# Merged loads, a rebalanced first batch and keep-warm matmuls in a spectral-mixing and MLP kernel on one core

## The chip, the cores and the metric

The kernel runs on one core of a Trainium2 chip. The metric is device time in microseconds (us) for one execution, taken as the median of several executions. A ratio is always the mean time of one kernel's runs over the mean of the other kernel's runs of the same rounds. It is therefore not quite the ratio of the medians that are quoted beside it. Intervals are 95%.

Engine names in the profile: PE is the tensor engine (matmul), PEld its weight loads, DVE the vector engine, ACT the scalar engine, POOL the GpSimd engine, SP the sync engine that issues stores.

## The reference

There are eight sequences of 3008 tokens with 256 channels. Each is filtered in the frequency domain along the tokens, and an MLP with a leaky ReLU of slope 0.01 follows. Inputs and output are float32; the kernel works in float16 with float32 sums.

```python
def _attn_ref(x, filt_r, filt_i):            # x: 8 x 3008 x 256
    X = np.fft.rfft(x, axis=1)
    F = (filt_r + 1j * filt_i)[None, :, :]   # 1505 x 256
    y = np.fft.irfft(X * F, n=x.shape[1], axis=1)
    return y.astype(np.float32)

def _moe_ref(x, w_in, w_out):                # x: 24064 x 256, w_in: 256 x 2048
    h = x @ w_in
    g = np.maximum(0.01 * h, h)
    return (g @ w_out).astype(np.float32)
```

## The kernel before

The transform of 3008 points is split as 94 x 32 (`N1` x `N2`). For each batch there is a first DFT over `n1` (matmuls with `f1_sb`), a transpose on DVE (`t1_part`), a second DFT over `n2` with the product by the filter, an inverse over `n2`, another DVE transpose (`t2_part`), and the last inverse DFT (`sb_group`) into `yts`. The MLP then runs in chunks of 512 tokens: `moe1_group` makes `h` on PE and its gate on ACT, and `moe2_slice` makes the output. Batches 1 to 7 are transformed beside the MLP of the batch ahead. Batch 0 has nothing to run beside, so it has its own path, in two halves of 128 channels each, and that path is what the change is about. Here are its loads, its steps and its order.

```python
def x_load(b, n0=0, nn=N2, d0=0, dn=D):
    src = x[b].rearrange("(n1 n2) d -> n1 n2 d", n2=N2)
    for lo, cnt in ((0, 64), (64, N1 - 64)):              # two transfers: 64 and 30 rows
        nc.gpsimd.dma_start(x_sb[lo : lo + cnt, ds(n0, nn), ds(d0, dn)],
                            src[lo : lo + cnt, ds(n0, nn), ds(d0, dn)])

def filt_load(dst, src, d0, dn):
    h = N2 // 2
    for s in range(2):                                    # four transfers of 16 rows
        q = s * Q
        nc.gpsimd.dma_start(
            dst[q : q + h, :, ds(d0, dn)], rows(src, NC * s, N1, 1, h, NC, d0, dn))
        nc.gpsimd.dma_start(
            dst[q + h : q + Q, :, ds(d0, dn)], rows(src, N1 - NC * s, N1, -1, h, NC, d0, dn))
# ... [cut] ...
def first_s2(hf, g, on_pool):                             # second DFT and products, 8 k1 columns
    ps = php.tile([P, W, DH], FP32, tag="ph", name=f"f2_h{hf}_g{g}")   # php: two PSUM slots
    # ... [two matmuls into ps] ...
    if on_pool:
        # ... [xs, y allocated] ...
        for j in range(2):
            nc.scalar.copy(xs[j][:], ps[:, ts(j, 4), :])  # ACT copies, POOL multiplies
        for i in range(2):
            for j in range(2):
                nc.gpsimd.tensor_tensor(y[i][:, ts(j, 4), :], xs[j][:], fs[i][:, ts(j, 4), :], AL.mult)
    else:
        # ... [y allocated] ...
        for i in range(2):
            nc.vector.tensor_tensor(y[i][:], ps[:], fs[i], AL.mult)    # DVE reads PSUM

def upper(hf):                                            # filter to the upper partitions
    for t, cp in ((fa_sb, nc.scalar.copy), (fb_sb, nc.vector.tensor_copy)):
        cp(t[64:P, :, ts(hf, DH)], t[0:64, :, ts(hf, DH)])

ac = (nc.scalar.copy, nc.scalar.copy)
first_front(0, copies)                                    # first DFT of a half, then t1
upper(0)
first_s2(0, 0, False), first_s2(0, 1, True)
first_s2(0, 2, False)
first_sa(0, 0, ac)                                        # inverse over n2
first_front(1, ac)
x_load(1)
first_sa(0, 2, ac), first_sa(0, 1, ac)
upper(1)
first_s2(1, 0, False), first_s2(1, 1, True)
# ... [w_out load] ...
first_s2(1, 2, False)
first_sa(1, 0, ac)
for i in range(2):
    t2_part(0, i)()
first_sa(1, 2, ac), first_sa(1, 1, ac)
for i in range(2, 4):
    t2_part(0, i)()
for g in range(16):                                       # last inverse DFT
    sb_group(0, g, copies[g % 2 if g >= 8 else 0], two[(g // 2) % 2])()
```

## Time and profile before

| | before |
|---|---|
| median of the first job's runs | 794.77 us (794.16 to 795.11, 4 runs) |
| profiled span | 793.3 us |
| first moe matmul / first gate activation | 45.70 / 47.60 us |
| transposes of batch 1 start | 61.09 us |
| last output copy starts | 789.04 us |

PE is busy for 96% of the span, and by the prediction's reading everything that can move lies ahead of about 68 us. The prediction, two sections on, shows the busy shares, the windows and the chain of work. These are the waits in the stretch from 26 to 36 us before the change: the engine and line that waited, what released it, then the total in us, the number of waits and the longest.

```profile
POOL fy_h_g L267 <- ACT fx_h_g L264: 4.1, 1, 4.1
DVE big L189 <- ACT big L177: 3.9, 1, 3.9
...
PE f_h_g L257 <- ACT fx_h_g L264: 1.6, 1, 1.6
DVE fy_h_g L271 <- ACT fa_sb L290: 1.4, 1, 1.4
```

DVE waits twice in this stretch, once for ACT's casts (3.9 us) and once for ACT's copy of the filter (1.4 us).

### The profile page before, as it was taken

How to read it: one execution, taken by the hardware profiler on the slowest of the kernel's cores; microseconds unless marked ns; L12 is line 12 of the kernel's file. 1: busy time of each engine (PE TensorE's matmuls, PEld its weight loads, DVE VectorE, ACT ScalarE, POOL GpSimd, SP SyncE). 2: the span in 40 equal slices, each digit the busy share in tenths (PEclk: the TensorE clock that was granted, in tenths of full speed). 3: DMA queues.
4: the chain of work that ended last, by engine and by line, in shares of the span. 5: the costliest groups of instructions: out<-in, count | busy, mean ns of one | idle time of the engine just before them, and what ended most of it. 6: DMA issues, size and time to landing. Idle time of an engine off the chain costs nothing.

```text
span 793.3 us, 13469 instructions
## 1 busy us (share of the span) xinstructions
PE 762.5 (96%) x5740; PEld 526.6 (66%) x5740; DVE 361.3 (46%) x448; ACT 561.2 (71%) x804; POOL 158.3 (20%) x138
## 2 busy tenths in 40 slices
PE   3688999999999999999999999999999999999997
PEld 2255677666776667866778667776677666676665
DVE  4728751675407743376414763077431765200000
ACT  3786768777596766877677776877769676666663
POOL 8763500141002500033000420024000340000000
PEclk9889999999999999999999999999999999999999
DMA  9934100501114010410105010151100101101111
GB/s 174 206 46 91 37 32 27 119 29 38 42 40 99 33 40 28 89 57 28 40 28 118 27 41 34 34 108 38 41 27 28 40 27 41 40 28 40 40 40 54
DMA packets 42300, 43.16 MB, mean 54 GB/s; under 512 B 14574, under 2 KB 40814, under 8 KB 41582
## 3 DMA queue, kind: packets, MB, share of 16 engines
q0 software_dynamic: 16048, 16.76, 13.0%
q1 hardware_dynamic: 26192, 25.53, 9.2%
q8 instruction: 45, 0.74, 0.4%
q14 instruction: 15, 0.12, 0.1%
HBM read 33.64 MB, written 24.64 MB: 73 GB/s over the span
## 4 chain that ended last, share of the span: by engine, by line
PE 91%; ACT 4%; DVE 3%; DMA 1%; issue 0%; POOL 0%; ACTq 0%; DVEq 0%; POOLq 0%
PE po_ps L348 40%; PE h_c_g L334 40%; PE sb_b_g L233 3%; PE s_b_g L166 3%; PE s_b_g L206 2%; PE sa_b_g L221 2%; ACT big L177 2%; DVE big L189 1%; DVE big L197 1%; PE o_c_t L348 1%; DMA x_sb<-in_x_dram 1%; ACT gt_c L339 1%; DVE fy_h_g L271 1%; PE f_h_g L257 0%; ACT fa_sb L290 0%
## 5 line engine op out<-in xcount | busy, mean ns | idle before, releaser
L339 ACT ACTIVATE gt_c<-h_c_g 128x1024 f16<-128x1024 f32 x376 | 385.6, 1026 | 196.7 <-PE h_c_g L334 195.7
L334 PE MATMUL h_c_g<-yt,w_in_sb 128*128 128x512 f16 (+7 forms) x1728 | 387.6, 352 | 1.3 <-ACT gt_c L339 1.0
L348 PE MATMUL po_ps<-w_out_sb,gt_c 128*128 128x256 f16 x2944 | 381.4, 272 | 0.6 <-ACT ost_c_t L355 0.6
L348 PEld LDWEIGHTS <-gt_c 128*128 128x128 f16 x3008 | 290.6, 98 | 88.7 <-issue 3.8
L334 PEld LDWEIGHTS <-w_in_sb 128*128 128x128 f16 x1728 | 163.3, 98 | 96.7 <-issue 2.8
L214 POOL TENSOR_TENSOR y_b_g<-p_b_g,p_b_g 128x512 f16<-128x512 f32 x84 | 106.9, 1273 | 222.3 <-DVE p_b_g L212 222.3
L189 DVE STREAM_TRANSPOSE big<-big 128x1024 f32<-128x1024 f32 x32 | 55.7, 1844 | 145.8 <-ACT big L177 145.7
L236 DVE CAST yt<-sb_b_g 128x376 f16<-128x376 f32 x116 | 58.5, 545 | 90.4 <-PE sb_b_g L233 90.2
L210 DVE TENSOR_TENSOR p_b_g<-s_b_g,fa_sb 128x512 f32<-128x512 f32 x84 | 58.1, 692 | 37.3 <-PE s_b_g L206 33.0
L355 ACT COPY ost_c_t<-po_ps 128x256 f32<-128x256 f32 x184 | 69.4, 377 | 7.4 <-PE po_ps L348 6.3
L197 DVE STREAM_TRANSPOSE big<-big 128x1024 f32<-128x1024 f32 x32 | 58.4, 1937 | 34.2 <-ACT big L177 34.2
L122 POOL DMA_DIRECT2D x_sb<-in_x_dram x22 | 13.9, 637 | 263.2 <-PE s_b_g L166 262.3
L177 ACT CAST big<-s_b_g 128x512 f16<-128x512 f32 x112 | 61.5, 621 | 0.0
L211 DVE TENSOR_TENSOR p_b_g<-s_b_g,fb_sb 64x512 f32<-64x512 f32 x84 | 58.2, 693 | 1.1
L212 DVE TENSOR_TENSOR p_b_g<-s_b_g,fb_sb 64x512 f32<-64x512 f32 x84 | 57.4, 684 | 1.1
L177 ACT CAST big<-sa_b_g 128x512 f16<-128x512 f32 x84 | 50.6, 602 | 0.0
L233 PEld LDWEIGHTS <-big 128*128 128x128 f16 x512 | 29.7, 101 | 17.7 <-DVE big L197 3.8
L233 PE MATMUL sb_b_g<-i_sb,big 128*128 128x94 f16 x512 | 33.3, 210 | 3.6 <-DVE big L197 3.2
L166 PE MATMUL s_b_g<-x_sb,f_sb 94*128 94x256 f16 x224 | 35.0, 276 | 1.3 <-ACT big L177 0.5
L206 PE MATMUL s_b_g<-big,small_sb 128*128 128x512 f16 x84 | 31.8, 379 | 1.8 <-DVE big L189 1.8
L221 PE MATMUL sa_b_g<-y_b_g,small_sb 128*128 128x512 f16 x84 | 31.8, 379 | 0.0
L166 PEld LDWEIGHTS <-f_sb 94*128 94x128 f16 x224 | 21.3, 99 | 11.9 <-issue 4.0
(37 smaller groups left out, 135.3 us busy)
## 6 DMA issues: line engine op xcount, KB each, us to landing
out_dram<-ost_c_t SPq DMA_DIRECT2D x92, 256.0 KB, 2.1
x_sb<-in_x_dram POOLq DMA_DIRECT2D x7, 1024.0 KB, 8.0
x_sb<-in_x_dram POOLq DMA_DIRECT2D x7, 480.0 KB, 10.2
x_sb<-in_x_dram POOLq DMA_DIRECT2D x4, 256.0 KB, 6.2
w_in_sb<-in_moe_w_in_dram POOLq DMA_DIRECT2D x1, 1024.0 KB, 9.6
w_out_sb<-in_moe_w_out_dram POOLq DMA_DIRECT2D x1, 1024.0 KB, 9.7
f_sb<-fwd_const SPq DMA_DIRECT2D x4, 192.0 KB, 3.4
fa_sb<-in_filt_r_dram POOLq DMA_DIRECT2D x8, 96.0 KB, 6.2
```

The lines of the kernel that those rows point to most:

```text
L166: nc.tensor.matmul(ps[:, j, :], f1_sb[:N1, n2, :], x_sb[:N1, n2, :], start=True, stop=True)
L177: copy(paired(dst)[:, ds(n0, nn), ds(e0, de)], ps[:].rearrange("p n (e t) -> p n e t", t=2))
L189: nc.vector.transpose(o, a)
L197: nc.vector.transpose(o[:, i // 2, ts(i % 2, E4), :], a)
L211: nc.vector.tensor_tensor(p2[0:64], ps[64:P], fb[64:P], AL.mult)
L214: nc.gpsimd.tensor_tensor(y1[:], p1[:], p2[:], AL.add)
L233: nc.tensor.matmul(ps[:, j, :], src[:, dt, n2, :], i1_sb[:, n2, :], start=True, stop=True)
L236: copy(yv[:, :, ds(4 * h, 4)], ps[:].rearrange("p c a -> p a c"))
L334: nc.tensor.matmul(ph[:, j, ds(o, ln)], w_in_sb[:, dt, ts(ct, P)], yts[b % 2][:, dt, ds(lo, ln)], start=(dt == 0), stop=(dt == NDT - 1),)
L339: nc.scalar.activation(gts[ci][:, ds(2 * g, 2), :], ph[:], AF.Lrelu)
L348: nc.tensor.matmul(po, gts[ci][:, ct, ts(tj, P)], w_out_sb[:, ct, :], start=(ct == 0), stop=(ct == NCT - 1))
L355: nc.scalar.copy(ost[:, tj % 2, :], po)
```

## The change

The intent has three parts. The filter rows of both sets of k1 (the frequency index of the first DFT) are laid side by side and x is loaded in 96 rows, so that 14 DMAs instead of 26 do the work up to the weights. The casts and products of the first batch are spread differently over ACT, DVE and POOL. Eight matmuls into an unused PSUM tile keep the tensor engine's clock up ahead of the last inverse DFT. The core of the diff follows; the reordered DFT constants and some allocation lines are cut.

```diff
     def x_load(b, n0=0, nn=N2, d0=0, dn=D):
-        src = x[b].rearrange("(n1 n2) d -> n1 n2 d", n2=N2)
-        for lo, cnt in ((0, 64), (64, N1 - 64)):
-            nc.gpsimd.dma_start(x_sb[lo : lo + cnt, ds(n0, nn), ds(d0, dn)],
-                                src[lo : lo + cnt, ds(n0, nn), ds(d0, dn)])
+        for lo, cnt in ((0, R1),) if b + 1 < B else ((0, 64), (64, N1 - 64)):
+            nc.gpsimd.dma_start(
+                x_sb[lo : lo + cnt, ds(n0, nn), ds(d0, dn)],
+                bass.AP(tensor=x.tensor, offset=x.offset + (b * N + lo * N2 + n0) * D + d0,
+                        ap=[[N2 * D, cnt], [D, nn], [1, dn]]))
 
     def filt_load(dst, src, d0, dn):
-        h = N2 // 2
-        for s in range(2):
-            # ... [two transfers of 16 rows each] ...
+        for q, first, sgn in ((0, 0, 1), (Q, N1, -1)):
+            nc.gpsimd.dma_start(
+                dst[q : q + Q, :, ds(d0, dn)],
+                bass.AP(tensor=src.tensor, offset=src.offset + first * D + d0,
+                        ap=[[N1 * D, N2 // 2], [sgn * NC * D, 2], [sgn * D, NC], [1, dn]]))
# ... [cut: first_s2 takes a first column c and a width n of 4 or 8; first_sa likewise] ...
+    def keep_warm(n):
+        for _ in range(n):
+            nc.tensor.matmul(po_ps[:].rearrange("p a d -> p (a d)"), small_sb[:, 0, :],
+                             i1_sb[:].rearrange("p a d -> p (a d)")[:, 0:512],
+                             start=True, stop=True)
 
-    ac = (nc.scalar.copy, nc.scalar.copy)
-    first_front(0, copies)
+    for g in range(8):
+        first_s1(0, g, two[(g // 2) % 2], (act, dve)[g % 2])
+    t1_part(0, 0, True)(), t1_part(0, 1, True)()
     upper(0)
-    first_s2(0, 0, False), first_s2(0, 1, True)
-    first_s2(0, 2, False)
-    first_sa(0, 0, ac)
-    first_front(1, ac)
+    first_s2(0, 0, 8, False)
+    first_s2(0, 8, 8, True)
+    first_s2(0, 16, 4, False)
+    first_s2(0, 20, 4, True)
+    for g in range(8):
+        first_s1(1, g, two[0], dve if g in (1, 3, 6) else act)
     x_load(1)
-    first_sa(0, 2, ac), first_sa(0, 1, ac)
+    t1_part(0, 2, True)(), t1_part(0, 3, True)()
+    first_sa(0, 0), first_sa(0, 16)
     upper(1)
-    first_s2(1, 0, False), first_s2(1, 1, True)
+    first_s2(1, 0, 8, False)
+    first_s2(1, 8, 8, True)
     nc.gpsimd.dma_start(w_out_sb[:], moe_w_out.rearrange("(ct p) d -> p ct d", p=P))
-    first_s2(1, 2, False)
-    first_sa(1, 0, ac)
-    # ... [t2 and inverse groups as before] ...
-    for g in range(16):
-        sb_group(0, g, copies[g % 2 if g >= 8 else 0], two[(g // 2) % 2])()
+    first_sa(0, 8), first_sa(0, 20)
+    first_s2(1, 16, 8, False)
+    first_sa(1, 0)
+    t2_part(0, 0)(), t2_part(0, 1)()
+    first_sa(1, 16), first_sa(1, 8)
+    t2_part(0, 2)(), t2_part(0, 3)()
+    keep_warm(5)
+    for g in range(8):
+        sb_group(0, g, act, two[(g // 2) % 2])()
+    keep_warm(3)
+    for g in range(8, 16):
+        sb_group(0, g, (act, dve)[g % 2], two[(g // 2) % 2])()
```

## The prediction

> **What bounds the kernel now.** I read the busy shares first. PE is busy 96% of the span, and its idle slices are all at the start. So I split the span in three windows: before the first moe matmul (45.7 us), up to the first product of batch 1 (68.4 us), and the rest.
>
> ```profile
> PE   3688999999999999999999999999999999999997
> PEclk9889999999999999999999999999999999999999
> ...
> 5.00:45.70 40.70, 23.87 (x164) 13.47 (x165) 27.81 (x26) 25.47 (x42) 33.67 (x34) 0.87 1.34 188
> 45.70:68.40 22.70, 18.54 (x93) 9.50 (x93) 7.56 (x5) 18.65 (x28) 8.47 (x3) 0.92 0.35 69
> 68.40:793.30 724.90, 720.05 (x5484) 503.61 (x5483) 324.93 (x416) 515.64 (x732) 112.24 (x94) 1.00 0.16 46
> ```
>
> The columns of a window are its bounds, length, busy us of PE, weight loads, DVE, ACT and POOL, the granted clock, the mean DMA share and GB/s. In the last 725 us PE is busy for 720. The change takes no matmul out of that part, so those 725 us stay. All that can move is the 68.4 us ahead of it. I read these from the chain of work that ended last, in order of time (start, us, what):
>
> ```profile
> 21.55 5.75 ACT big L177 x12
> ...
> 28.10 2.76 ACT fa_sb L290
> ...
> 30.89 4.62 DVE fy_h_g L271 x4
> 35.50 7.22 DVE big L197 x4
> ...
> 42.77 2.39 PE sb_b_g L233 x28
> ...
> 45.70 1.88 PE h_c_g L334 x4
> ...
> 60.58 0.49 ACT big L177
> ...
> 61.09 7.23 DVE big L189 x4
> ```
>
> Up to 21.5 the loads and batch 0's first half set the pace. Then come ACT's casts, ACT's copy of the filter to the upper partitions, DVE's products, DVE's transposes, the last inverse DFT, and four moe matmuls. From 47.6 to 61.1 the chain is ACT without a gap (a gate activation, then three casts of batch 1, over and over). DVE's transposes of batch 1 follow, and at 68.4 PE saturates. Nothing in 47.6 to 68.4 is changed. So what matters is one number: **how much earlier than 47.60 does the first gate activation start**, and all of it should reach the end.
>
> **What the Trainium skill says.** "DMA: Bandwidth & Descriptors", Rules for kernel authors, says that two transfers to disjoint partition halves serialize on the same 16 engines and gain nothing over one. Its section "Why a DMA increments its semaphore by 16 and not by 1" says the engines used are at most 16 and divide the slowest dimension, so 96 rows use 16 and a 30-row remainder 15. The trace agrees in that the traffic is flat at 173 to 183 GB/s from 6 to 22 us whether 64, 30 or 16 rows travel; a gain from 15 to 16 engines can't be seen. "TensorE: Matmul & The Clock Gate", Part 1, says PE runs at half clock after an idle window of some 3.4 us and at full clock after as long a busy one, with a free-running window. This trace agrees: 128x512 matmuls start 0.42 us apart at 20 us, about 0.24 at 36 us, and the first four moe matmuls take 1.88 us against 0.86 us later. The clock around them:
>
> ```profile
> 42.00:44.00 2.00, 1.23 (x17) 1.24 (x17) 1.10 (x2) 1.25 (x4) 2.00 (x1) 0.58 1.43 195
> 44.00:46.00 2.00, 1.75 (x20) 1.43 (x18) 1.77 (x4) 1.34 (x3) 2.00 (x1) 0.50 0.21 28
> 46.00:48.00 2.00, 2.00 (x7) 0.89 (x6) 0.04 (x1) 0.40 (x1) 2.00 (x1) 0.50 0.00 0
> ```
>
> **Part 1: fewer loads.** Up to the weights, POOL issues 26 transfers (8 of x, 16 of filter, 2 of weights); after the change 14. Its issue row costs 0.72 to 1.03 us for a half-x transfer and about 0.6 for a filter one, hardly by size, so 12 fewer save some 12 x 0.6 = 7 us of POOL. The timeline of POOL shows what that is worth:
>
> ```profile
> 7.81 0.59 POOL L135 DMA_DIRECT2D fb_sb<-in_filt_i_dram  x1 [0.90 <-DMA x_sb<-in_x_dram]
> ...
> 21.07 0.72 POOL L152 DMA_DIRECT2D w_in_sb<-in_moe_w_in_dram  x1
> 21.89 2.29 POOL L267 TENSOR_TENSOR fy_h_g<-fx_h_g,fa_sb 128x512 f16<-128x512 f32 x2
> ```
>
> The ninth transfer waits until the first lands, the tenth for the second, and so on: eight seem to be allowed in flight. With doubled transfers the issuing is ahead and ends near 15.6 us (worked out with those landings), so POOL's first products start when ACT's copies are there (18.2) instead of 21.9. But the bytes are the same (x +2%) and the engines were saturated anyway. The first x half lands at 10.4 us, the second at 13.6 + 6.0 = 19.6, first-half filters near 15.5. I let all three stand. Direct gain: about 0; it makes part 2 possible. In the steady state x loads are hidden, so 0 there too.
>
> **Part 2: rebalanced first batch.** Before, the second half's first DFT stood behind two inverse groups on PE and ACT, and all eight casts were ACT's. DVE idled 3.93 us until 26.13. Now the half follows directly once PE is free of the first-half products (19.7, x landed at 19.6). I walk it:
> - DVE ends the first products at 19.2; the new half-size pair takes 2 x 0.69 (the row of 512-element products) to 20.6. ACT copies POOL's extra half group by 20.35.
> - Eight groups: PE makes one per 0.43 us cold, ACT casts five (0.51 to 0.59 each), DVE three (0.69). The sixth, the third of DVE's, ends at 23.5; ACT's last at about 23.8. Transposes start at 23.5 to 23.8, against 26.13: 2.4 us earlier.
> - But DVE's next products waited for ACT's filter copy (2.75 us, ended 30.86), not for the transposes. ACT now does three inverse casts first, 1.6 us warm to 2.5 cold (PE gives one per 0.85), so the copy starts at 25.4 to 26.3 and ends at 28.2 to 29.0. Gain **1.9 to 2.7**.
> - From there DVE's 4.62 us of products and 7.22 us of transposes stand. POOL's second-half products end at about 33.6 (4 x 1.14 after ACT's copy), their inverse casts at 35.5 to 37.6, before or about when the third transpose starts (36.5 to 37.2). At most 0.4 is lost if PE is cold.
>
> So the transposes end at 40.0 to 40.9 instead of 42.72; I take **2.1 us**.
>
> **Part 3: keep-warm matmuls.** Eight 128x512 matmuls cost 8 x 0.216 = 1.7 us warm, 3.4 cold. Before, PE waits 1.98 us for the transposes ahead of the inverse DFTs and 1.19 us between their halves. Five fit in the first gap if warm (1.1 us), as do three in the second (0.65). Worth: from the end of the transposes to the gate activation it is 42.72 to 47.60 = 4.9 us now. Warm, the four moe matmuls take 0.86 instead of 1.88 (1.0 us), and the last inverse groups become bound by DVE's four casts (4 x 0.61 after 0.4, so 2.85 us, with the moe matmuls beginning under the last), some 0.4 shorter: about **1.4 us** if the clock holds, 0 if not. I give warmth 7 in 10, so 1.0 us, and charge 0.1 for the chance that cold fillers delay the inverse DFTs.
>
> Sum: 2.1 + 1.0 - 0.1 = 3.0; with both at their better end 4.1, at their worse end 1.5. Warmth is also likelier where PE's work has moved together, so I take 3.3.
>
> **Rivals.** (a) The DMA sets the start: the second x half lands later than 19.6, or transfers of 1536 pieces start more slowly. For it: the DMA is full from 2 to 22 us. Against: it is first in, first out, and the order is the same. It would leave about 1 to 2 us, some 793. (b) PE becomes the bound of the first 45 us: the fillers or the new order run cold and push the inverse DFTs, whose first half needs ACT for 8 x 0.39 to 0.47 us and just ends (42.7) when the transposes do. A delay of 1 us there costs about 1 us: some 793 again. (c) The shift is swallowed later, by ACT's chain to 61 or by x of batch 1. Against: that load is issued at about 25 and lands by 38, and ACT has no idle to absorb. (d) The steady state changes. Against: same matmuls, hidden loads; no effect in 725 us of saturated PE.
>
> **The range and the chances.** 794.66 - 3.3 = 791.4. The better end with some luck in the clock gives 4.6 less, 790.0; (a) or (b) give up to 793.2. Two per cent are 15.9 us, a third of the whole first part, so it stays within 2% almost for sure: 0.985, faster 0.01, slower 0.005.
>
> **What would show it right or wrong.** POOL's first product before 19 us and its last weights issue near 15.6 (part 1). The second-half transposes near 23.7, the second filter copy ending near 28.6, the last transpose of batch 0 near 40.6 (part 2). A clock of 0.9 or more from 40 us and first moe matmuls of about 0.9 us (part 3). Batch 1's transposes 13.5 us after the first gate activation, and the saturated part still 725 us long. I would be wrong if the x landings move, if the fillers end after the second transpose, or if the saturated part changes length.

## The result

| | before | after |
|---|---|---|
| median of the first job's runs | 794.77 us (794.16 to 795.11) | 792.40 us (792.09 to 793.09) |
| ratio | | 0.9972 (0.9955 to 0.9989) |
| profiled span | 793.3 us | 790.6 us |
| first moe matmul / first gate activation | 45.70 / 47.60 us | 44.73 / 45.99 us |
| last output copy starts | 789.04 us | 787.42 us |
| from there to the end | 4.23 us | 3.22 us |

The output is correct. The time fell by 2.4 us (medians; 2.2 by the ratio), inside the predicted range and within the 2%. Of the 2.7 us between the two spans, 1.6 us lies ahead of the gate activation and 1.0 us lies in the **last four microseconds**, which the prediction never mentions.

The busy rows and the windows of the kernel after answer to those that the prediction shows of before. In the windows, the columns are again bounds, length, busy us of PE, weight loads, DVE, ACT and POOL, then granted clock, DMA share and GB/s.

```profile
PE   2788999999999999999999999999999999999998
...
PEclk9999999999999999999999999999999999999999
...
5.00:45.70 40.70, 25.06 (x176) 13.95 (x176) 29.37 (x29) 24.55 (x40) 30.20 (x23) 1.00 1.35 191
45.70:68.40 22.70, 18.17 (x102) 9.69 (x100) 8.36 (x6) 18.66 (x28) 6.46 (x2) 1.00 0.36 70
68.40:790.60 722.20, 718.44 (x5474) 502.46 (x5471) 323.76 (x415) 515.61 (x732) 110.08 (x90) 1.00 0.16 46
```

The first PE digit is lower than before (2 for 3): the first matmul starts at 9.29 us instead of 8.32, as x landed later in this execution. The granted clock reads 1.00 in all three windows, where it was 0.87 and 0.92 in the first two. Read this column with care: the trace has no clock record ahead of the first rise, at 23.3 us here and 21.8 us before, and the view counts that time as full speed. The matmuls show that it was not: the first DFT's 128-column matmuls start 107 ns apart until that moment and 55 ns apart after it. What went away is the half-speed stretches after the first rise. In the saturated part PE works as densely as before. From the first gate activation to the last output copy there are 741.4 us in both profiles, so the saturated part carries a front shift through unchanged.

The chain of work that ended last after the change (start us, us, what) answers to the chain in the prediction:

```profile
26.62 2.76 ACT fa_sb L282
...
29.41 2.37 DVE fy_h_c L269 x2
31.77 0.05 issue
31.82 1.04 PE f_h_c L253 x2
32.85 0.02 issue
32.88 2.36 DVE fy_h_c L269 x2
35.23 7.28 DVE big L194 x4
...
45.15 0.82 PE h_c_g L339 x3
...
59.49 7.24 DVE big L186 x4
```

ACT's filter copy starts at 26.62 instead of 28.10, so that part of the change works. But DVE's four products, a single piece of 4.62 us before, are now two pieces of 2.37 and 2.36 with **two matmuls between them**. The transposes (7.28 us) start at 35.23 instead of 35.50, and the gain of 1.5 us is nearly gone. The waits from 26 to 36 us say why. These lines answer to the waits shown of before:

```profile
PEld L253 <- DVE fy_h_c L269: 1.8, 1, 1.8
...
PE f_h_c L253 <- DVE fy_h_c L269: 1.3, 1, 1.3
...
DVE fy_h_c L269 <- PE f_h_c L253: 1.1, 1, 1.1
```

PE waits for DVE's products, then DVE waits 1.1 us for PE. My reading: the third group of the second half now takes over the PSUM slot that DVE's own first group is still reading, not the slot that ACT had emptied, so that DVE and PE take turns on one slot. An experiment below tests it. In every unedited execution profiled, and in every variant that kept the slot, the second group starts at least 3.47 us after the first, against 2.27 us before.

### The profile page after: what moved, and what is told of

Its sections match the earlier page's. It is cut to its first block, busy times and chain, and to the rows that moved or that the text cites. A ratio compares the mean times of both kernels' runs of the same rounds, so it can differ in the third digit from the quotient of the medians. Undisturbed runs are those within 1.5% of the kernel's fastest.

```text
span 790.6 us, 13456 instructions
## 1 busy us (share of the span) xinstructions
PE 761.7 (96%) x5748; PEld 526.2 (67%) x5748; DVE 362.5 (46%) x451; ACT 560.3 (71%) x802; POOL 150.6 (19%) x122
## 4 chain that ended last, share of the span: by engine, by line
PE 92%; ACT 3%; DVE 3%; DMA 1%; issue 0%; POOL 0%; ACTq 0%; DVEq 0%; POOLq 0%
PE po_ps L353 40%; PE h_c_g L339 40%; PE sb_b_g L230 3%; PE s_b_g L163 3%; PE s_b_g L203 2%; PE sa_b_g L218 2%; ACT big L174 2%; DVE big L186 1%; DMA x_sb<-in_x_dram 1%; DVE big L194 1%; PE o_c_t L353 1%; ACT gt_c L344 1%; DVE fy_h_c L269 1%; PE f_h_g L244 1%; PE f_h_c L253 1%
## 5 line engine op out<-in xcount | busy, mean ns | idle before, releaser
L125 POOL DMA_DIRECT2D x_sb<-in_x_dram x12 | 8.5, 713 | 263.0 <-PE s_b_g L163 262.2
```

## The experiments

All runs below gave correct outputs, and each was timed in five rounds (the one with cut filter transfers has six runs) against the kernel before on the same chip. Three jobs of four kernels were run. The kernel before had medians of 794.78, 794.73 and 794.63 us in them (9, 11 and 9 runs), so numbers can be compared across jobs through the ratios. "Gate" is the first gate activation in the profile, and "tail" runs from the start of the last output copy to the end. At the threshold of 2% every run's verdict is "same".

| run | median us | ratio to before (95%) | gate us | tail us |
|---|---|---|---|---|
| after, again | 792.68 | 0.9970 (0.9957 to 0.9982) | 46.38 | 3.22 |
| after without fillers | 793.48 | 0.9983 (0.9970 to 0.9995) | 46.77 | 3.22 |
| before with fillers | 793.78 | 0.9987 (0.9974 to 1.0001) | 46.86 | 3.90 |
| after, other PSUM slot | 791.46 | 0.9957 (0.9944 to 0.9969) | 45.06 | 3.22 |
| after, x in 64 + 32 rows | 793.25 | 0.9978 (0.9965 to 0.9990) | 46.92 | 3.21 |
| after, filter transfers cut in two | 795.27 | 1.0008 (0.9994 to 1.0023) | 49.39 | 3.26 |
| after, both cut | 794.18 | 0.9995 (0.9984 to 1.0007) | 49.02 | 3.26 |
| after, x in quarters | 792.17 | 0.9970 (0.9959 to 0.9982) | 45.40 | 3.23 |
| after, longer POOL work | 792.73 | 0.9982 (0.9970 to 0.9995) | 46.18 | 3.24 |
| before + 8 tiny ACT instructions | 793.82 | 0.9988 (0.9976 to 1.0001) | 47.55 | 3.21 |
| after + 4 tiny ACT instructions | 794.12 | 0.9994 (0.9980 to 1.0007) | 45.55 | 4.18 |
| other slot + x in quarters | 790.87 | 0.9953 (0.9940 to 0.9965) | 44.39 | 3.22 |

The differences are of the order of 1 us in 790, and the intervals are 2 us wide. So each verdict rests on the profile's milestones as well as on the time. My theory was this: the rebalancing gains about 2 us and loses 1.1 us of it to the PSUM slot, the fillers gain about 1 us, and the end of the kernel gains 1 us for a reason outside the change's intent. The rivals were that the merged transfers land later by their size, that fewer transfers are the gain, and that the fillers do nothing.

### The changed kernel once more

No edit. It tells which of the first profile's details are the kernel's and which are that execution's.

> The changed kernel once more, unedited, to size the whole effect and the end of the span. The profile of it moved the start of the first gate activation by 1.61 us (47.60 to 45.99) and the last output copy by 1.62, but its span by 2.7; the rest would be the last store's landing (1.7 against 2.4 us). Theory: the time gained is the front's 1.6 us plus chance in that last store, so 1.6 to 2.0 us over five rounds (ratio 0.9975 to 0.998). Rival: the tail is shortened for a reason of the change, and the gain stays at 2.4 or more (0.997 or less).

It took 792.68 us, and the ratio of 0.9970 and the tail of 3.22 us fit the rival and not the theory: the short tail came twice, so chance is unlikely. The slot wait is there again at 1.12 us. The late x load of the first profile is not: the second x piece's matmuls begin at 10.85 us, against 11.59 us there and 10.52 us before. The granted clock has one half-speed stretch (33.2 to 36.6 us), where the first profile had none. The Trainium skill, "TensorE: Matmul & The Clock Gate", Part 1, says that the window that sets the clock is free-running and that the warm-up differs between runs. These two profiles agree: the first rise of the clock is at 23.3 us in one and 26.4 us in the other.

### After without the fillers, and before with them

```diff
-    keep_warm(5)
     for g in range(8):
         sb_group(0, g, act, two[(g // 2) % 2])()
-    keep_warm(3)
```

> The changed kernel without its eight filler matmuls. Theory: the fillers hold PE's clock; without them it falls to 0.5 somewhere from 40 to 48 us, the first four moe matmuls take some 1.9 us, and the first gate activation starts at 47.3 instead of 45.99: 1.3 us lost. Rival: the closer order alone keeps PE warm, the clock stays at 1.0 and nothing is lost (0 +- 0.3 us).

The second kernel is the one before with the same `keep_warm` calls at the same two places (5 and 3), and `po_ps` allocated earlier for them.

> The kernel before with the same 5 + 3 fillers and nothing else. Theory: they alone are worth what the prediction gave them, the first gate activation starts 1.2 to 1.5 us ahead of 47.60 and the time falls by as much, with the transposes still ending at 42.7. Rival: PE is cold when they come (clock 0.5 from 29 to 35 us), they take 0.43 us each and push the inverse transforms: 0 to 0.5 us gained.

These are 793.48 and 793.78 us. Both theories have the mechanism and overstate the size: 0.8 us lost in time for an expected 1.3, and 0.74 us gained at the gate for 1.2 to 1.5. Without the fillers the clock falls at 42.6 us, much as it did before (42.3), and stays down for 3.4 us where it stayed down for 6.8. The windows of the changed kernel without fillers come first:

```profile
42.00:44.00 2.00, 1.47 (x20) 1.48 (x21) 1.09 (x3) 1.31 (x4) 2.00 (x1) 0.66 0.63 84
44.00:46.00 2.00, 1.75 (x17) 1.25 (x16) 1.58 (x3) 1.04 (x3) 2.00 (x1) 0.50 0.00 0
```

The same windows of the unedited kernel after, which answer to those in the prediction:

```profile
42.00:44.00 2.00, 1.41 (x28) 1.30 (x29) 1.39 (x3) 1.53 (x5) 2.00 (x1) 1.00 0.73 99
44.00:46.00 2.00, 1.73 (x14) 0.87 (x12) 1.09 (x3) 0.64 (x3) 2.00 (x1) 1.00 0.04 5
46.00:48.00 2.00, 1.86 (x12) 0.97 (x11) 0.00 (x0) 2.00 (x4) 2.00 (x1) 1.00 0.01 4
```

From the end of the transposes to the gate, the three profiles without fillers (before, after without, and before with tiny ACT instructions) have 4.89, 4.30 and 4.33 us. Ten of the eleven profiles with fillers have 3.49 to 3.52 us and the other 3.79 us. In all eleven the granted clock is full from 42 to 50 us; in none of the three without fillers is it. The fillers are therefore worth 0.8 to 1.4 us on the path, and 0.8 us between the two medians of the same job (793.48 and 792.68). Alone on the kernel before they gave 1.0 us in time and 0.74 us at the gate; the tail of that run is 0.33 us shorter as well.

### The other PSUM slot

Two pools of one buffer each stand in for the pool of two, and a small class hands them out in turn unless told which. Three calls name their slot, two of them to keep what they had. Only the third one's slot differs from the changed kernel's.

```diff
-    php = ctx.enter_context(tc.tile_pool(name="php", bufs=2, space=bass.MemoryType.PSUM))
+    ph_pools = [ctx.enter_context(tc.tile_pool(name=f"ph{i}", bufs=1, space=bass.MemoryType.PSUM))
+                for i in range(2)]
+    # ... [class Slots: hands out the pools in turn, or the slot that is asked for] ...
-    first_s2(0, 16, 4, False)
-    first_s2(0, 20, 4, True)
+    first_s2(0, 16, 4, False, 1)
+    first_s2(0, 20, 4, True, 0)
-    first_s2(1, 16, 8, False)
+    first_s2(1, 16, 8, False, 0)
```

With the original slot for that third call, the wrapper builds a program with the same slots and the same order of instructions as the changed kernel's. That was compared in the program and not run. The trace of the run speaks for it too: up to the slot it keeps the times of the repeat (second-half transposes at 24.38 us against 24.41, DVE's first product at 29.71 against 29.74).

> The changed kernel with one PSUM slot chosen otherwise: the last product group of the second half takes the slot that ACT's copy has freed and not the one that DVE's products still read. Theory: DVE's wait of 1.12 us ahead of that group goes (it would start at 31.8 instead of 32.88), the transposes end near 41.4 instead of 42.51, and the first gate activation and the time come 1.0 to 1.1 us earlier. Rival: something else is as late (ACT's inverse casts or POOL's products ahead of the third transpose), and under 0.4 us is gained.

It took 791.46 us, 1.2 us less than the unedited kernel of the same job (1.0 us in the means; all five of its runs, 791.00 to 791.62, lie below all five of the repeat, 791.65 to 793.09). The chain of this run:

```profile
26.92 2.76 ACT fa_sb L293
...
29.71 4.62 DVE fy_h_c L280 x4
34.33 7.25 DVE big L205 x4
```

The products are one piece of 4.62 us again. In the waits from 26 to 36 us the line for PE is back in its old form, the last release coming from ACT's copies, and it costs DVE nothing:

```profile
PE f_h_c L264 <- ACT fx_h_c L272: 0.8, 1, 0.8
```

The transposes end at 41.57 us against 42.88. The wait on the slot is thus **shown** to cost 1.1 us on the path, and some 1.0 to 1.2 us of time. Why the pool of two hands out the other slot in the changed order was not looked into.

### The size of the x and filter transfers

Three kernels cut the merged transfers again: x of batch 0 in 64 + 32 rows, each merged filter transfer in two of 16 partitions, and both. A fourth keeps 96 rows but loads x in quarters of `n2`, each half as large.

```diff
-        for lo, cnt in ((0, R1),) if b + 1 < B else ((0, 64), (64, N1 - 64)):
+        for lo, cnt in ((0, 64), (64, 32)) if b == 0 else ((0, R1),) if b + 1 < B else ((0, 64), (64, N1 - 64)):
```

> The changed kernel with the first batch's x in eight transfers again (64 and 32 rows, the same bytes), the filters still merged. Theory (size): a transfer of 1536 pieces starts and lands later than two of 1024 and 512, so the first matmul comes back from 9.29 to about 8.3 us, the first transpose from 14.29 to about 13.3, and the time falls by about 1.0 us. Rival (crowding): x is late because the merged filter transfers come right behind it and take their share of the DMA engines; then the first matmul stays at 9.0 to 9.3 and the time stays.

```diff
-            nc.gpsimd.dma_start(
-                dst[q : q + Q, :, ds(d0, dn)],
-                bass.AP(tensor=src.tensor, offset=src.offset + first * D + d0,
-                        ap=[[N1 * D, N2 // 2], [sgn * NC * D, 2], [sgn * D, NC], [1, dn]]))
+            for k in (0, 8):
+                nc.gpsimd.dma_start(
+                    dst[q + 2 * k : q + 2 * k + 16, :, ds(d0, dn)],
+                    bass.AP(tensor=src.tensor, offset=src.offset + (first + N1 * k) * D + d0,
+                            ap=[[N1 * D, 8], [sgn * NC * D, 2], [sgn * D, NC], [1, dn]]))
```

> The changed kernel with each merged filter transfer cut in two of 16 partitions, x still merged. Theory (size of the x transfer): the first matmul stays at about 9.3 us; the issues on POOL go on longer (its first product still near 19.4, as ACT's copy sets it) and the time is the same within 0.4 us. Rival (crowding): with eight transfers in flight there is less filter traffic behind x, and the first matmul comes back to 8.3 to 8.6, the time falls by 0.7 to 1.0 us.

The third has both edits.

> Both cut: the 26 transfers of before in the changed kernel's order of work. This is the rebalancing and the fillers without the merging. Theory: first matmul at 8.3 us; POOL's issues end near 21.8 again and its first product waits for them (21.9 instead of 19.4), but as that product's inverse groups are used late the transposes of the first batch end no later than 41.5, and the time is 1.0 us under the changed kernel's. Rival: POOL's late products delay its second-half ones or the casts, and the gain of the earlier x is lost (0 +- 0.3 us).

```diff
-        for n0 in (0, N2 // 2):
-            x_load(0, n0, N2 // 2, hf * DH, DH)
+        for n0 in range(0, N2, 8):
+            x_load(0, n0, 8, hf * DH, DH)
```

> The changed kernel with the first batch's x in eight transfers cut the other way: 96 rows of 8 columns each (768 pieces), so that no 30- or 64-row transfer is in it and a quarter of the data allows a quarter of the groups. Theory (size): the first matmul comes at 8.0 us or before, as half as many pieces have to land; the last x of the half lands near 10.4, the transposes start at 13.3, 1.0 us gained. Rival (the 96-row shape itself is slow to start): the first matmul comes at 8.8 or later, the transposes at 14.0 or later, and less than 0.4 us is gained.

**Rows make no difference that shows.** With 64 + 32 rows the second x piece's matmuls begin at 10.78 us, with 96 rows at 10.85 in the repeat. Over the profiles with x in merged halves and filters as changed, the first transposes start at 13.40 to 14.29 us. In the three profiles of the kernel before and its variants it is 13.22 to 13.79. Neither the theory nor its rival came in: the lateness in the first profile was that execution's, not the transfer's. The run's 793.25 us is 0.6 us above the repeat, and its profile shows a long half-speed stretch instead, 33.7 to 40.5 us. There the fillers do what the prediction's rival (b) feared. In PE's timeline of this run (start us, us, engine, line) the five fillers take 2.25 us, and the inverse DFT behind them begins without a gap:

```profile
35.56 3.15 PE L277 MATMUL fa_h_c<-fy_h_c,small_sb 128*128 128x512 f16 x7 [0.52 <-DVE fy_h_c L269]
38.51 2.25 PE L287 MATMUL po_ps<-i_sb,small_sb 128*128 128x512 f16 x5
40.59 1.24 PE L230 MATMUL sb_b_g<-i_sb,big 128*128 128x94 f16 x24
```

In the first profile of the kernel after, at full clock, the same fillers leave a gap:

```profile
36.81 1.24 PE L287 MATMUL po_ps<-i_sb,small_sb 128*128 128x512 f16 x5
38.98 1.24 PE L230 MATMUL sb_b_g<-i_sb,big 128*128 128x94 f16 x24 [0.93 <-DVE big L194]
```

So where the half-speed stretch falls changes from execution to execution, and cold work on PE cost this one 0.3 us after the transposes (3.79 against 3.49) and 0.2 us inside them, where DVE waited 0.23 us for the casts of late inverse groups before its third transpose.

**The quarters bring x earlier.** The first matmul starts at 7.72 us instead of 8.34 to 9.29, and the first transposes at 13.09. The gate, 45.40 us, is ahead of the three unedited or tail-only profiles of the kernel after (45.55 to 46.38), by 0.6 us of their mean. The time alone, 792.17, would not have shown it.

**Cutting the filter transfers failed as a test of their number.** Both kernels are slower than the changed one (795.27 and 794.18 us), where an equal time and a gain of 1.0 us were expected, and two things that came with the cut show in the traces. First, the transfers lost rate. These windows of the run with cut filters have GB/s as the last column:

```profile
10.00:14.00 4.00, 3.15 (x29) 2.71 (x26) 2.43 (x4) 2.36 (x4) 2.20 (x4) 1.00 1.76 147
14.00:18.00 4.00, 1.03 (x3) 0.38 (x4) 3.45 (x4) 2.75 (x1) 4.00 (x5) 1.00 1.59 146
```

The changed kernel moves 180 and 182 GB/s in these windows. The Trainium skill, "DMA: Bandwidth & Descriptors", section "Why a DMA increments its semaphore by 16 and not by 1", says that the number of engines is the largest up to 16 that divides the slowest dimension of both sides. My cut made the source's slowest dimension 8. The lower rate agrees with that, and the runs do not show the engines used. Second, POOL's issuing now lasted until after 24 us, so its products started late and met DVE's copy of the other filter. POOL's and DVE's timelines of this run:

```profile
26.89 2.31 POOL L265 TENSOR_TENSOR fy_h_c<-fx_h_c,fb_sb 128x512 f16<-128x512 f32 x2
29.12 1.19 POOL L265 TENSOR_TENSOR fy_h_c<-fx_h_c,fa_sb 128x512 f16<-128x512 f32 x1
30.24 1.17 POOL L265 TENSOR_TENSOR fy_h_c<-fx_h_c,fb_sb 128x512 f16<-128x512 f32 x1
...
27.87 4.88 DVE L283 COPY fb_sb<-fb_sb 64x3072 f16<-64x3072 f16 x1
```

The same copy takes 0.95 us in the repeat of the changed kernel. Here it lasts 4.88 us, through several POOL instructions, and ends only after the last of them has ended and POOL has turned to issuing a transfer (31.33 us). "SBUF — State Buffer", section "Who interferes with whom", says that DVE in its two-port modes and GpSimd share a port pair exclusively, and that whoever issues first holds it for the whole instruction while the other blocks. The trace agrees, and shows a wait of several instructions. What the halved number of filter transfers is worth with everything else equal stays **open**: no run isolates it.

### Longer POOL work in the changed kernel

To see that interference by itself, POOL gets a memset and a scaling of an unused region between its two groups of first-half products. That puts a POOL instruction across DVE's copy.

```diff
+    nc.gpsimd.memset(yts[1][0:64, 0, 0:1600], 0.0)
+    nc.gpsimd.tensor_scalar(yts[1][0:64, 0, 0:1600], yts[1][0:64, 0, 0:1600], -1.0, None, AL.mult)
     first_s2(0, 16, 4, False)
```

> The changed kernel with about 4 to 6 us of needless work on POOL (it clears and scales a scratch stretch) between its two groups of first-half products, transfers untouched. It makes POOL late, as the uncut number of transfers did in the two runs with split filters. Theory: DVE's copy of the imaginary filter (0.95 us alone) can't run beside POOL's tensor operations, so it stretches until POOL pauses for the x load, from 0.95 to 3 us or more; DVE's second-half products start 0.8 to 2 us later and the time rises by 0.8 to 2 us. Rival: the split runs were slow by their transfers (x or filters landing late), POOL's lateness itself is hidden, the copy stays at 0.95 to 1.3 us and the time within 0.4 us.

POOL's and DVE's timelines of this run:

```profile
24.51 4.25 POOL L298 TENSOR_SCALAR yt<-yt 64x1600 f16<-64x1600 f16 x1
28.76 1.82 POOL L264 TENSOR_TENSOR fy_h_c<-fx_h_c,fa_sb 128x512 f16<-128x512 f32 x1
...
26.70 2.88 DVE L282 COPY fb_sb<-fb_sb 64x3072 f16<-64x3072 f16 x1
```

The copy is stretched from 0.95 to 2.88 us. POOL's next product, 1.15 us elsewhere, takes 1.82 and ends some 0.7 us later than it would. So the stretching is shown (that a shared port is its reason is what the skill says, not what this run shows), but my expectation of its cost, 0.8 to 2 us, was missed. ACT's own filter copy ended at 29.26 us, so DVE's stretched copy (29.58) cost the path only about 0.35 us. The median, 792.73 us, equals the repeat's; the ratio is higher because one of the five runs took 794.84 us.

### The last four microseconds

The tail is 4.23 us before and 3.22 us after, and no line of code there differs. What differs is an 8 KB fetch in the "instruction" queue that the profile lists among the DMA queues. These are the GB/s row and the last stores' median time to landing for the stretch 786 to 794 us, 40 slices of 0.2 us, of the kernel before:

```profile
GB/s 0 0 0 10 302 297 31 26 20 10 0 0 36 323 287 10 0 0 0 0 0 154 333 128 41 0 20 10 10 0 0 0 0 0 0 0 0 41 0 0
...
out_dram<-ost_c_t SPq DMA_DIRECT2D x3, 128.0 KB, 2.4
```

The last store (154, 333, 128) has moved 123 KB by the end of its third slice. Then comes the fetch, 8 KB in one slice (41 GB/s x 0.2 us), and after a gap the store's last 8 KB at 20, 10 and 10 GB/s. Eight KB is a sixteenth of the store, as much as one of the core's 16 DMA engines would carry if all shared it evenly. So it looks as if one engine's share waited for the fetch; the trace lists queues and not engines, so this step is not shown. After the change:

```profile
GB/s 0 0 0 0 41 348 261 5 0 0 0 0 0 210 353 92 0 0 0 0 0 0 0 0 41 0 0 0 0 41 0 0 0 0 0 0 0 0 0 0
...
out_dram<-ost_c_t SPq DMA_DIRECT2D x2, 128.0 KB, 1.7
```

Here the store (210, 353, 92) is complete, and the fetch follows 1.6 us later and disturbs nothing. The theory is that the fetch is triggered by the count of instructions that an engine has run, and ACT's stream is four instructions shorter after the change (958 in the trace against 962). Two kernels test it by adding one-element activations near the start, where ACT is idle, eight to the kernel before and four to the one after:

```diff
     nc.scalar.activation(one[:], one[:], AF.Lrelu)
+    for _ in range(8):              # 4 in the kernel after
+        nc.scalar.activation(one[:], one[:], AF.Lrelu)
```

> The kernel before with eight more one-element activations on ACT at 2 us, where ACT is idle. They cost nothing in the front. Theory: the end of the span holds an 8 KB fetch of ACT's instructions on the queue 'instruction', which in this kernel falls 1.9 us after the last output copy starts, into the last store (over at 2.66 instead of 1.75 us); eight instructions more move it ahead of or behind that store, the stretch from the last copy to the end falls from 4.2 to 3.2 us and the time by 0.7 to 1.0 us, with the first gate activation still at about 47.6. Rival: that stretch varies by chance or by the number of POOL's instructions; it stays at 3.9 to 4.2 and the time stays.

> The changed kernel with four more one-element activations on ACT at 2 us, so that ACT has as many instructions as in the kernel before (962 in the trace). Theory: the fetch of ACT's instructions falls into the last store as there; the stretch from the last copy to the end grows from 3.2 to 3.9 to 4.2 us and the time by 0.7 to 1.0. Rival (POOL's count or the transfers decide): 3.2 us as in all runs of the changed kernel, the time the same.

The same view of before with eight more, then, in a second fence, of after with four more:

```profile
GB/s 0 0 0 87 343 200 10 15 20 20 0 0 113 364 180 0 0 0 0 0 0 287 328 41 0 0 0 0 0 0 0 0 41 0 0 0 0 0 0 0
...
out_dram<-ost_c_t SPq DMA_DIRECT2D x3, 128.0 KB, 1.7
```

```profile
GB/s 0 0 133 348 174 0 0 0 0 0 0 271 302 41 41 10 15 15 0 0 0 0 0 0 0 0 0 41 0 0 0 0 0 0 0 0 0 0 0 0
...
out_dram<-ost_c_t SPq DMA_DIRECT2D x2, 128.0 KB, 2.2
```

Both signs came out. With 970 ACT instructions the kernel before has a tail of 3.21 us and is 0.8 us faster (793.82 against 794.63; the interval of the ratio just reaches 1). With 962 the kernel after has a tail of 4.18 us and takes 794.12 us, about 1.5 us more than its repeat (whose before was 794.78 where this one's was 794.63). That is more than the 0.96 us of the tail. Its five runs spread over 1.8 us, so the excess is not resolved. The tail follows ACT's count and nothing else that I varied. The kernel before with fillers has 962 again and a tail of 3.90 us; the run without fillers has fewer PE instructions and the same short tail, and POOL's count is the same in the kernel after with either tail.

### Both improvements

The other slot and x in quarters together.

> The changed kernel with the PSUM slot of the fourth run and x in quarters (96 rows of 8 columns). Theory: the two add up, as one is in the loads and one behind them: x in quarters brought the transposes of the first half 0.3 to 0.5 us forward, the slot 1.1 us; the first gate activation starts at 44.2 to 44.8 and the time is 0.3 to 0.6 us under the slot's alone, some 0.9953 of before. Rival: the gain of the quarters was the clock's phase, which varies from run to run, and the time is the slot's alone, 0.9957.

It took 790.87 us, ratio 0.9953 (0.9940 to 0.9965), with the gate at 44.39 us. It is the fastest kernel. Beside the slot alone it gains 0.6 us in the median (0.3 by the ratios, as the kernel before was faster in this job too) and 0.67 at the gate; the intervals of the two ratios overlap, so this second gain rests on the profiles.

## Why the prediction was right or wrong

The total was right: 792.4 us measured against 791.4 predicted, in a range up to 793.2. The composition was not, and the total owes its place in the range to luck (the last point below).

| term | predicted us | measured us | from |
|---|---|---|---|
| loads (direct) | 0 | -0.3 | first transposes: 13.77, mean of 3 profiles after, against 13.46, mean of 2 before; chance |
| ACT's filter copy, relative to the first transposes | 1.9 to 2.7 | 2.1 (1.5 to 2.5) | 14.87 (mean of 2) to 12.82 (mean of 3) |
| PSUM slot | not seen | -1.1 to -1.2 | gap between the product groups; undone by the other slot |
| end of batch 0's transposes | 2.1 | 0.5 | 42.97 (mean of 2) to 42.48 (mean of 3) |
| fillers | 1.4 if warm | 0.8 to 1.4 | 4.30 to 4.89 without, 3.49 with |
| first gate activation | 3.3 | 1.6 | 47.58 (mean of 2) to 45.97 (mean of 3) |
| tail | not seen | 1.0 | 4.23 to 3.22 |

The "after" profiles are the first, the repeat and the one with four tiny ACT instructions; the "before" ones are the first and the one with eight.

- **Part 1.** The direct gain of about 0 held. POOL's weights issue was at 16.45 us in the first profile and 15.50 in the repeat for a predicted 15.6, and its first product at 19.40 in the first profile and 18.66 in the repeat, where "before 19 us" was asked. ACT's copies released it, as predicted, and no longer POOL's own issuing (21.89).
- **Part 2, first half.** The second-half transposes started at 24.92, 24.41 and 24.31 us in the three profiles, for a predicted 23.5 to 23.8. From the first transposes on, the step is nearly right: 12.9 us before and 10.6 to 10.9 after are 2.0 to 2.3 us gained for a predicted 2.4. The filter copy ended at 29.0 to 29.7, at the late edge of "28.2 to 29.0" or beyond it, in part by the late start. How long after the first transposes it starts differs by 1.1 us between the three profiles (12.3, 12.7 and 13.4 us), in the order in which the clock first rose in them (23.3, 24.5 and 26.4 us): what looks like a fixed step holds a part that changes from execution to execution.
- **The step that failed** is "From there DVE's 4.62 us of products and 7.22 us of transposes stand." I had walked engines and queues but not PSUM slots. In the kernel before, the same two slots served the three groups without holding up DVE, and I took that to hold. In the changed order the third group waits for DVE's own first group, so DVE's products take 5.8 us from first to last instead of 4.62. The run with the other slot shows the products whole again, and the transposes ending at 41.57 us, 1.3 us earlier than in the repeat.
- **Part 3.** The mechanism was right, and against the kernel before so was the size: from the end of the transposes to the gate 1.4 us are gained (4.89 to 3.49). The split was not. Of these 1.4 us, 0.8 lie ahead of the first moe matmul, for a predicted 0.4, and 0.6 in the moe matmuls, for a predicted 1.0: they end 1.24 us after they start in the chain, for a predicted 0.9 and 1.88 before. The chance of 7 in 10 was too low: full clock from 42 us on in eleven profiles of eleven. The rival (b) is real but small, seen in one run with a long cold stretch. The last step of the sum, from 3.0 to 3.3 because warmth was "likelier", had no number behind it.
- **The carry-through** was right: 13.5 us from the gate to batch 1's transposes and 741.4 us from the gate to the last copy, in every run.
- **What made the total look right** is the tail: 1.0 us from four ACT instructions fewer, which has nothing to do with the change's intent. Without it the time would have been about 793.4 us (an estimate, 792.4 + 1.0), beyond the 793.2 of the range, and the kernel with the count put back took 794.1. Where both kernels have the short tail (the repeat, and before with eight tiny instructions) the ratios put the change at 1.4 us; where both have the long one they put it at 0.5 us. The gate says 1.6 us. The runs do not settle it more closely than that.

## What to carry to other kernels

When a reordering lets an engine start earlier, write down for each buffer slot which reader must finish before the next writer, as well as each engine's own queue: a pool of two can hand the third tile the slot of the first reader or of the second, and here that choice was worth 1.0 to 1.2 us. When a change of 2 us in 790 is to be explained, compare the last microseconds of both traces too, because the mere count of instructions can move a fetch into or out of the last store. A few throw-away matmuls in a gap that PE waits through anyway are cheap while the clock is up, and in all eleven profiles with them here it was up from 42 us on.

## What the Trainium skill lacked or had wrong

- "Runtime: NRT & Kernel Launch", section "Instruction fetch mechanics", calls the cost of crossing an instruction block mostly hidden. In the last four microseconds it is not: where an 8 KB fetch fell into the last store, the store's last 8 KB came after it and the tail was 4.18 to 4.23 us instead of 3.21 to 3.22. No page that I read has this.
- "SBUF — State Buffer", section "Who interferes with whom", says that the loser of the shared port pair blocks for the other's whole instruction. When POOL's instructions follow each other without a gap, the loser waited through several: a DVE copy of 0.95 us took 4.88 us.
- "TensorE: Matmul & The Clock Gate", Part 1, gives about 216 ns between 512-column matmuls at full clock. Contiguous operands agree here (six in 1.47 us). The second DFT, whose moving operand is read in strided pairs, needs twice that at a granted clock of 1.00: four in 1.88 us at 27.34 us of the first profile of the kernel after. It is no slower ahead of the clock's rise (two in 1.02 us at 18.78 us of the kernel before, two in 1.04 us at 31.82 us after), so this step gains nothing from a warm clock. The page's spacing has no term for strides, and what the skill says of strided SBUF reads elsewhere gives no figure for a matmul.
